# Second block of a three-part kernel: when the copies of block products stand, which steps use block products, and where the side work goes

## Chip, cores and metric

One Trainium2 chip, one core. The metric is the device time of one launch in microseconds (us). The clock of the matmul engine has two levels, 1.2 and 2.4 GHz; the profile gives the granted level as a share of the higher one.

## The reference

```python
def _attn_ref(q, k, v, g_norm):
    kv = np.einsum('bhsd,bhse->bhde', k, v)
    out = np.einsum('bhsd,bhde->bhse', q, kv)
    rms = np.sqrt(np.mean(out * out, axis=-1, keepdims=True) + 1e-06)
    return (out / rms * g_norm).astype(np.float32)

def _moe_ref(x, w_in, w_out):
    h = x @ w_in
    g = np.maximum(0.01 * h, h)
    return (g @ w_out).astype(np.float32)

def _moe2_ref(x, w_in, w_out, a, b):
    h = x @ w_in
    h2 = h * h
    h3 = h2 * h
    P = a[0] + a[1] * h + a[2] * h2 + a[3] * h3
    Q = 1.0 + np.abs(b[0]) * np.abs(h) + np.abs(b[1]) * h2
    g = P / (Q + 1e-06)
    return (g @ w_out).astype(np.float32)
```

The result of the attention part (batch 8, 8 heads, 576 positions, head size 64), laid out as 4608 rows of 512, goes through `_moe_ref` (the first block, inner width 2048) and then through `_moe2_ref` (the second block, the same widths). All is float32.

## The kernel before

**Tiling.** The 4608 rows are 9 chunks `c` of 512. The inner width of 2048 is 16 slices `f` of 128. Every float32 operand is held as a pair of float16 values, high and low, and a product is three float16 matmuls (`mm3`, L433 to L435). An instruction order written out by hand is kept on every engine; a wait between engines is set wherever an instruction touches a tile that another engine wrote or read.

**The second block** (L1313 to the end) runs 9 chunks of 8 steps `j`; a step makes slices 2j and 2j+1 of `h` in one accumulator tile of two banks, `ph` (two such tiles in turn), then the rational function `g` of them. It also runs one pair of slices of the second matmul, `y`, from a step made earlier: `y_steps2(n)` takes n pieces off a list `pend` as long as it holds more than `lag` slices. A piece is 3 matmuls of 512 columns, and 8 pieces are a pair of slices.

**The rational function** (`rational`, L1316) is, on ScalarE (ACT), three reads of `ph` into `e`, `s`, `p` (L1324 to L1326), and `z` (two instructions, L1332 and L1333); on VectorE (DVE), `d1` (L1335, from `s` and `e`), `d2` and `d3` (L1337, L1338, from `p` and `ph`), and `d4` to `d6` (L1339 to L1341, from `e`, `z`, `p`). Its last part `g` is a high half by ScalarE (L302) and a low half by GpSimd (POOL, L297).

**Plain and block steps.** A plain step makes `h` by 24 matmuls of 512 columns (`emit_h`, twice 12). A block step (`by_parts`, odd `j`) makes it out of seven block products in the manner of Strassen and Winograd, each 6 matmuls of 256 columns. The text numbers them in their order: 1 is A11 x B11, 2 is A12 x B21, 3 is S2 x T2, 4 is S1 x T1, 5 is S3 x T3, 6 is S4 x B22, 7 is A22 x T4. Four quarters `q0` to `q3` of the tile `ph` take them (`q0`, `q1` in the first bank, `q2`, `q3` in the second): products 1, 3, 5 and 7 go to `q0`, product 2 to `q2`, 4 and 6 to `q3`. ScalarE copies `q0` after product 1 (`m`, L1511) and after 3 (`u`, L1518), and `q3` after product 4 (`v`, L1522). VectorE then adds `m` to `q2` (L1515), `v` and `q0` into `q1` (L1526), and `u` to `q3` (L1532). Block steps before: j = 5 and 7 of chunk 1, and all odd steps of chunks 2 to 8 but the last of all: 29.

In a block step the code stands as follows, with `r` the rational function of the plain step before it:

```python
product2(q0, j, kc, "A11", "B11", True)
nc.scalar.copy(out=m, in_=q0)
product2(q2, j, kc, "A12", "B21", True)
y_steps2(3)
run(r, "z d2")
nc.vector.tensor_tensor(out=q2, in0=m, in1=q2, op=ALU.add)
run(r, "d3")
```

The rational function of the block step itself (`fresh`) is run in the plain step that follows.

**Side work.** Block steps need sums of the operands: of the weights, per odd j, a load (`load_sums`), four sums on VectorE (`sum_w2`, L1412) and two conversions (`form_w2`); of the next chunk's rows, four sums `T1` to `T4` (L1453) with four conversions on each of ScalarE and VectorE (`H`, `L`, L350 and L352), besides the conversions of the rows themselves (`h`, `l`, same lines). `plan` says at which step each is put. The scales of the last chunk (`x_scales`, L238 to L292, 14 short parts that go back and forth between ScalarE and VectorE) all stand at step 6 of chunk 1.

Of the kernel before, what the change touches and what calls it, by code (L numbers as in the profile page):

```python
# [9 lines left out]
F32 = mybir.dt.float32  # L10
# [10 lines left out]
P = 128  # L21
# [27 lines left out]
def kernel(  # L49
# [489 lines left out]
    with tc.manual_schedule():  # L539
# [809 lines left out]
        steps, evac, fresh, half, late = [], [], [], [], []  # L1349

        def y_steps2(n):
            for _ in range(n):
# [6 lines left out]
                if pf == p0 and e == 0:  # L1359
                    assert not evac  # L1360
                    Y[pc] = new_y()
# [97 lines left out]
        FILLS = ("h0 T1", "h1 l0 T2 T3", "h2 h3 l1", "H1 H2 l2 l3 T4", "H3 L1", "H4 L2 L3", "L4")  # L1459
# [4 lines left out]

        for c in range(NCH - 1):
            for n, f in enumerate(FILLS):
                for x in f.split():
                    put(c, min(n + (2 if c == 0 else 1), NP - 1), x[0] not in "hH", x_item, c + 1, x)
        for j, c, n in ((5, 0, 1), (7, 0, 3), (1, 1, 0), (3, 1, 2)):
            for i in range(2):  # L1470
                put(c, n + i * (c == 0), 1, sum_w2, j, i)
            for i in range(2):
                put(c, n + 1 + (c == 0) + i, i, form_w2, j, i)
        ask_w2 = {(0, 0): 5, (0, 1): 7, (0, 6): 1, (1, 0): 3}
# [5 lines left out]
        def by_parts(c, j):  # L1480
            return j % 2 and (c > 1 or c == 1 and j > 4) and (c, j) != (NCH - 1, NP - 1)

        lag = 4
        for c in range(NCH):
            kc = NCH + c
            if c == 1:
                lag = 6
            for j in range(NP):
                ph = ps_h2.tile([P, 2, N], F32, tag="h2", name="ph2")
# [3 lines left out]
                if final:  # L1493
                    late.pop(0)["g"](False)
                    for i in range(2):
                        if i:
                            ph = ps_h2.tile([P, 2, N], F32, tag="h2", name="ph2")
                        emit_h(2 * j + i, ph[:, i, :], X[kc], W2)
                        r = rational(c, ph, gt, i, i + 1)
# [65 lines left out]
                if c == 1 and j == 3:  # L1565
                    asked = spread_sums(x_norms(NCH - 1, 1), dqx, 1)
                if c == 1 and j == 6:
                    reduce(wrk["n"][:, NCH - 1:NCH], asked, ALU.add)
                    for *_, fn in x_scales(wrk["n"][:, NCH - 1:NCH], NCH - 1, 1):
                        fn()  # L1570
# [49 lines left out]
```

## Time and profile before

| | |
|---|---|
| median of 3 runs | 1604.55 us (1603.87 to 1605.08) |
| profiled execution: its time | 1603.33 us |
| its span, first to last instruction | 1601.5 us |
| PE / DVE / ACT / POOL busy | 1545.5 / 1223.5 / 990.3 / 190.1 us |
| mean granted clock | 0.993 |
| chain that ended last | PE 61%, DVE 23%, ACT 8%, DMA 4% |

Busy times are sums over an engine's instructions. PE is the matmul engine. Its busy share of 97% counts slow and overlapped matmuls too, so what it loses is read from the stretches in which it started nothing, and from the starts of its steps.

### The profile page before, as it was taken

To read this page: it belongs to the slowest core of one execution; us is meant where nothing else is said; L and a number is where in the kernel's file an instruction comes from. 1 tells how busy PE (TensorE), PEld (TensorE's weight loads), DVE (VectorE), ACT (ScalarE), POOL (GpSimd) and SP (SyncE) were. 2 spreads that over 40 slices of the span, in tenths; PEclk is the share of its full clock that TensorE was granted. 3 is DMA by queue.
4 is the path that set the end of the run, shared out by engine and by line. 5 is a ranking of instruction groups with operands and counts; after the bars stand their busy time and mean duration, and the time that the engine had idled before them with its cause. 6 is when DMAs were issued, how large, how long until landed. Compare 5 with 4: busy or idle time off the path is not lost.

```text
span 1601.5 us, 22684 instructions
## 1 busy us (share of the span) xinstructions
PE 1545.5 (97%) x9156; PEld 901.8 (56%) x9156; DVE 1223.5 (76%) x1658; ACT 990.3 (62%) x1404; POOL 190.1 (12%) x136
## 2 busy tenths in 40 slices
PE   9999999999999999999999978999999999999998
PEld 5888754445666666666644434555555555555553
DVE  6787466766765767665679998989889898989776
ACT  6567645544545555545767666767677776767665
POOL 0000000000110101000011221122221221222220
PEclk9999999999999999999999989999999999999999
DMA  8454623140534434323321010101010100100000
GB/s 320 120 185 148 172 95 93 66 119 21 186 126 125 158 116 128 100 85 106 118 79 55 1 55 1 53 1 53 1 53 1 42 12 7 47 1 27 1 27 27
DMA packets 44205, 125.26 MB, mean 78 GB/s; under 512 B 4932, under 2 KB 5316, under 8 KB 44100
## 3 DMA queue, kind: packets, MB, share of 16 engines
q1 hardware_dynamic: 35936, 96.42, 18.3%
q0 software_dynamic: 7200, 25.69, 5.2%
q10 hardware_dynamic: 964, 1.70, 0.5%
q8 instruction: 71, 1.16, 0.3%
q14 instruction: 34, 0.28, 0.1%
HBM read 92.34 MB, written 31.46 MB: 77 GB/s over the span
## 4 chain that ended last, share of the span: by engine, by line
PE 61%; DVE 23%; ACT 8%; DMA 4%; issue 4%; SPq 0%; POOL 0%; ACTq 0%; POOLq 0%; DVEq 0%
PE y L433 10%; PE y L434 10%; PE y L435 10%; PE ph L433 6%; PE ph L435 6%; PE ph L434 6%; DVE e L1335 3%; DVE p L1338 3%; DVE p L1340 2%; DVE p L1337 2%; DVE e L1339 2%; DVE x L352 2%; DVE p L1341 2%; PE chain L433 2%; ACT g L302 2%
## 5 line engine op out<-in xcount | busy, mean ns | idle before, releaser
L297 POOL TENSOR_TENSOR g<-p,g 128x1024 f16<-128x1024 f32 x70 | 156.8, 2240 | 731.2 <-ACT g L302 712.3
L435 PE MATMUL y<-g,v 128*128 128x512 f16 x576 | 219.6, 381 | 3.4 <-POOL g L297 3.4
L433 PE MATMUL y<-g,v 128*128 128x512 f16 x576 | 220.1, 382 | 0.0
L434 PE MATMUL y<-g,v 128*128 128x512 f16 x576 | 220.0, 382 | 0.0
L433 PE MATMUL ph<-x,v 128*128 128x512 f16 (+1 forms) x460 | 162.4, 353 | 41.6 <-ACT m L1511 37.5
L434 PEld LDWEIGHTS <-v 128*128 128x128 f16 x1094 | 107.4, 98 | 140.8 <-issue 43.9
L435 PEld LDWEIGHTS <-v 128*128 128x128 f16 x1094 | 107.5, 98 | 111.9 <-issue 2.1
L433 PE MATMUL y<-g,n 128*128 128x512 f16 x448 | 169.8, 379 | 0.0
L434 PE MATMUL y<-g,n 128*128 128x512 f16 x448 | 169.8, 379 | 0.0
L435 PE MATMUL y<-g,n 128*128 128x512 f16 x448 | 169.8, 379 | 0.0
L433 PEld LDWEIGHTS <-v 128*128 128x128 f16 x1094 | 107.5, 98 | 108.9 <-issue 5.7
L435 PE MATMUL ph<-x,v 128*128 128x512 f16 (+1 forms) x460 | 162.5, 353 | 0.0
L434 PE MATMUL ph<-x,v 128*128 128x512 f16 (+1 forms) x460 | 162.5, 353 | 0.0
L302 ACT ACTIVATE g<-p 128x1024 f16<-128x1024 f32 (+1 forms) x73 | 76.5, 1047 | 97.5 <-DVE p L1341 97.3
L435 PEld LDWEIGHTS <-n 128*128 128x128 f16 x816 | 79.7, 98 | 70.8
L1335 DVE SCALAR_TENSOR_TENSOR e<-s,b,e 128x1024 f32<-128x1024 f32 (+1 forms) x73 | 97.8, 1340 | 26.4 <-ACT s L1325 26.4
L433 PEld LDWEIGHTS <-n 128*128 128x128 f16 x816 | 79.9, 98 | 61.9 <-issue 5.6
L1332 ACT ACTIVATE z<-e,lnb 128x1024 f32<-128x1024 f32 (+1 forms) x73 | 83.1, 1138 | 47.3 <-DVE e L1335 47.1
L434 PEld LDWEIGHTS <-n 128*128 128x128 f16 x816 | 79.7, 98 | 56.8 <-issue 0.7
L1324 ACT ACTIVATE e<-ph,small 128x1024 f32<-128x1024 f32 (+1 forms) x73 | 79.7, 1092 | 31.7 <-DVE ph L1532 28.8
L1338 DVE SCALAR_TENSOR_TENSOR p<-p,small,ph 128x1024 f32<-128x1024 f32 (+1 forms) x73 | 92.3, 1264 | 1.6
L1340 DVE SCALAR_TENSOR_TENSOR p<-p,small,z 128x1024 f32<-128x1024 f32 (+1 forms) x73 | 92.3, 1264 | 0.0
(252 smaller groups left out, 3425.2 us busy)
## 6 DMA issues: line engine op xcount, KB each, us to landing
tmp<-in_w_dram SPq DMA_DIRECT2D x32, 512.0 KB, 7.1
raw<-in_kv_dram SPq DMA_DIRECT2D x25, 512.0 KB, 5.5
w<-in_w_dram POOLq DMA_DIRECT2D x22, 512.0 KB, 5.2
w<-cv SPq DMA_DIRECT2D x32, 256.0 KB, 3.2
raw<-w SPq DMA_DIRECT2D x16, 512.0 KB, 4.1
raw<-x SPq DMA_DIRECT2D x16, 512.0 KB, 4.3
out_dram<-raw SPq DMA_DIRECT2D x16, 512.0 KB, 2.9
sq<-rs SPq DMA_DIRECT2D x13, 512.0 KB, 6.6
```

Of the source, the lines that this page charges most:

```text
L297: (nc.gpsimd if pool else nc.vector).tensor_tensor(out=lo, in0=src, in1=hi if hi.dtype == F16 else hi.bitcast(F32), op=ALU.subtract)
L302: nc.scalar.activation(out=hi, in_=src, func=AF.Copy)
L352: nc.vector.scalar_tensor_tensor(out=lo, in0=src, scalar=scale, in1=hi, op0=ALU.mult, op1=ALU.subtract)
L433: nc.tensor.matmul(out=dst, lhsT=wl, rhs=xh, start=first, stop=False, **kw)
L434: nc.tensor.matmul(out=dst, lhsT=wh, rhs=xh, start=False, stop=False, **kw)
L435: nc.tensor.matmul(out=dst, lhsT=wh, rhs=xl, start=False, stop=last, **kw)
L1324: nc.scalar.activation(out=e, in_=ph, func=AF.Abs, scale=k["e"])
L1332: nc.scalar.activation(out=z[0], in_=e, func=AF.Abs_reciprocal_sqrt, scale=Q_S, bias=lnb[:, 1:2])
L1335: return {"d1": lambda: stt(out=e, in0=s, scalar=b1[:, 0:1], in1=e, op0=ALU.mult, op1=ALU.add), "z": root, "d2": lambda: nc.vector.tensor_ ...
L1337: "d2": lambda: nc.vector.tensor_tensor(out=p, in0=p, in1=ph, op=ALU.mult),
L1338: "d3": lambda: stt(out=p, in0=p, scalar=k["c1"], in1=ph, op0=ALU.add, op1=ALU.mult),
L1340: "d5": lambda: stt(out=p, in0=p, scalar=k["c0"], in1=z[0], op0=ALU.add, op1=ALU.mult),
```

## The change

Five things change, all in the second block.

1. In a block step the copies `m`, `u` and `v` are issued behind the next product: `m` behind product 2, and `u` and `v` together behind product 4, which now follows product 3 at once. The tile `vm` holds `v` and `m`, and one addition of 512 columns makes `q1` and `q2` behind product 5.
2. The `g` of a plain step that a block step follows moves from that block step into the plain step after it, behind `e`, `s`, `p`; there the conversions on ScalarE (`fill(c, j, 0)`) move behind `z`.
3. Block steps are used from chunk 2 on: 27. The sums of the rows of chunk 1 (`T`, `H`, `L`) are left out.
4. Side work: all weight sums and their loads stand in chunk 0, the norm of the last chunk is asked for at step 3 of chunk 0, and its 14 scale parts stand one to a step in chunks 2 and 3. The evacuation of the first block's last chunk (`after`) stands at the end of its step.
5. `lag` goes 4, 5, 6 where it went 4, 6, and in the last step 4 pieces of `y` stand behind each of the two `h`.

```diff
@@ y_steps2
-                    evac_y(ys, x2[pc], (nc.scalar, nc.scalar), x=pc, scale=sy1)
+                    after.append(lambda: evac_y(ys, x2[pc], (nc.scalar, nc.scalar), x=pc, scale=sy1))
@@ plan
-        for j, c, n in ((5, 0, 1), (7, 0, 3), (1, 1, 0), (3, 1, 2)):
+        for j, n in ((1, 0), (3, 1), (5, 3), (7, 4)):
...
+        put(0, 3, 1, last_norms)
+        put(0, 7, 1, sum_norms)
+        for i, (v, _, fn) in enumerate(x_scales(wrk["n"][:, NCH - 1:NCH], NCH - 1, 1)):
+            put(2 + i // NP, i % NP, v > 0, fn)
...
         def by_parts(c, j):
-            return j % 2 and (c > 1 or c == 1 and j > 4) and (c, j) != (NCH - 1, NP - 1)
+            return j % 2 and c > 1 and (c, j) != (NCH - 1, NP - 1)
...
+                lag = 4 if c == 0 else 5 if (c, j) == (1, 0) else 6
@@ last step
                         emit_h(2 * j + i, ph[:, i, :], X[kc], W2)
+                        y_steps2(NC)
...
-                    y_steps2(2 * NC)
@@ block step
-                    product2(q0, j, kc, "A11", "B11", True)
-                    nc.scalar.copy(out=m, in_=q0)
-                    product2(q2, j, kc, "A12", "B21", True)
+                    product2(q[:, 0, :], j, kc, "A11", "B11", True)
+                    product2(q[:, 2, :], j, kc, "A12", "B21", True)
+                    nc.scalar.copy(out=vm[:, 1, :], in_=q[:, 0, :])
                     y_steps2(3)
-                    run(r, "z d2")
-                    nc.vector.tensor_tensor(out=q2, in0=m, in1=q2, op=ALU.add)
-                    run(r, "d3")
-                    product2(q0, j, kc, "S2", "T2")
-                    nc.scalar.copy(out=u, in_=q0)
-                    y_steps2(1)
+                    run(r, "z d2 d3")
+                    product2(q[:, 0, :], j, kc, "S2", "T2")
+                    product2(q[:, 3, :], j, kc, "S1", "T1", True)
+                    nc.scalar.copy(out=u, in_=q[:, 0, :])
+                    nc.scalar.copy(out=vm[:, 0, :], in_=q[:, 3, :])
+                    y_steps2(2)
                     fill(c, j, 0)
-                    product2(q3, j, kc, "S1", "T1", True)
-                    nc.scalar.copy(out=v, in_=q3)
-                    y_steps2(1)
                     run(r, "d4 d5")
-                    product2(q0, j, kc, "S3", "T3")
-                    nc.vector.tensor_tensor(out=q1, in0=v, in1=q0, op=ALU.add)
+                    product2(q[:, 0, :], j, kc, "S3", "T3")
+                    nc.vector.tensor_tensor(out=q[:, 1:3, :], in0=vm, in1=ph[:, :, 0:HN], op=ALU.add)
...
-                    run(r, "d6 g")
+                    run(r, "d6")
+                    late.append(r)
                     fill(c, j, 1)
@@ plain step behind a block step
                         r = rational(*fresh.pop())
-                        fill(c, j, 0)
-                        fill(c, j, 1)
-                        run(r, "d1 " + REST)
+                        late.pop(0)["g"]()
+                        fill(c, j, 1)
+                        run(r, "d1 z")
+                        fill(c, j, 0)
+                        run(r, "d2 d3 d4 d5 d6")
```

On PE, where product 1 ends and product 2 begins, step 5 of chunk 2, before (`ph` is the accumulator, `x` the rows, `v` the weights):

```order
L435 LDWEIGHTS v_7354
L435 MATMUL ph_9178<-x_1_8213,v_7354 128x256
L433 LDWEIGHTS v_7354
L433 MATMUL ph_9178<-x_2_8214,v_7354 128x256 [waits Activation_49]
L434 LDWEIGHTS v_7354
```

and now:

```order
L435 LDWEIGHTS v_7354
L435 MATMUL ph_9080<-x_1_8211,v_7354 128x256
L433 LDWEIGHTS v_7354
L433 MATMUL ph_9080<-x_2_8212,v_7354 128x256
L434 LDWEIGHTS v_7354
```

Product 2 waited for ScalarE and no longer does. Three `y` pieces later, product 3 now has the wait:

```order
L435 MATMUL y_8919<-g_8812,v_7000 128x512
L433 LDWEIGHTS s_5_7951
L433 MATMUL ph_9080<-x2T_8440,s_5_7951 128x256 [waits Activation_49]
L434 LDWEIGHTS s_5_7951
L434 MATMUL ph_9080<-x2T_8440,s_5_7951 128x256
```

On ACT, steps 4 and 5 of chunk 2, before (`x2T` are conversions of sums of rows):

```order
L1326 ACTIVATE p<-ph_9001,small 128x1024 [waits Pool_49]
L350 ACTIVATE x2T_9129<-xsum,small 128x512
L350 ACTIVATE x2T_9131<-xsum,small 128x512
L1332 ACTIVATE z<-e,lnb 128x1024 [waits DVE_49]
...
L302 ACTIVATE g_9002<-p 128x1024 [waits DVE_49]
L1511 COPY m<-ph_9178 128x256 [waits PE_49]
L1332 ACTIVATE z<-e,lnb 128x1024 [waits DVE_49]
L1333 ACTIVATE z<-z 128x1024 [waits Activation_49]
L1518 COPY u<-ph_9178 128x256 [waits DVE_49,PE_49]
L350 ACTIVATE x2T_9221<-xsum,small 128x512
L1522 COPY v<-ph_9178 128x256 [waits PE_49]
L302 ACTIVATE g_9096<-p 128x1024 [waits DVE_49]
```

and now:

```order
L1326 ACTIVATE p<-ph_8900,small 128x1024 [waits Pool_49]
L302 ACTIVATE g_8812<-p 128x1024
L1332 ACTIVATE z<-e,lnb 128x1024 [waits DVE_49]
L1333 ACTIVATE z<-z 128x1024 [waits Activation_49]
L350 ACTIVATE x2T_9037<-xsum,small 128x512
...
L302 ACTIVATE g_8901<-p 128x1024 [waits DVE_49]
L1527 COPY vm<-ph_9080 128x256 [waits PE_49]
L1332 ACTIVATE z<-e,lnb 128x1024 [waits DVE_49]
L1333 ACTIVATE z<-z 128x1024 [waits Activation_49]
L1532 COPY u<-ph_9080 128x256 [waits PE_49]
L1533 COPY vm<-ph_9080 128x256
L350 ACTIVATE x2T_9131<-xsum,small 128x512
```

The `g` of the plain step before has moved ahead of `z`, the conversions behind it, and the two copies `u` and `v` stand together, still behind the next `z`.

## Rows read from the trace of the kernel before

**Rows 1.** Busy time by stretch: us, then PE, PEld, DVE, ACT, POOL, clock, DMA.
```profile
801.80:987.20 185.40, 165.74 (x780) 77.58 (x781) 169.91 (x182) 120.55 (x134) 31.87 (x15) 0.94 0.11 39
987.20:1570.40 583.20, 559.06 (x3129) 305.67 (x3127) 501.40 (x499) 416.24 (x476) 122.75 (x55) 1.00 0.07 22
1570.40:1601.50 31.10, 26.20 (x121) 11.50 (x119) 18.88 (x23) 13.55 (x19) 2.15 (x1) 0.99 0.09 34
```
**Rows 2.** Who waited for whom, 987.2 to 1570.4: total us, times, longest.
```profile
DVE ph L1532 <- PE ph L435: 29.2, 28, 1.6
...
PE ph L433 <- ACT m L1511: 24.1, 27, 1.5
```
**Rows 3.** Who waited for whom, 801.8 to 987.2.
```profile
PE ph L433 <- ACT m L1511: 13.3, 2, 6.8
...
PE y L435 <- POOL g L297: 3.4, 2, 2.0
...
PE ph L433 <- DVE p L1338: 2.9, 3, 2.1
```
**Rows 4.** Timeline of PE, chunk 2: start, us, idle before and its end.
```profile
1018.86 0.27 PE L435 MATMUL ph<-x,v 128*128 128x256 f16 x1
1020.61 0.27 PE L433 MATMUL ph<-x,v 128*128 128x256 f16 x1 [1.48 <-ACT m L1511]
...
1029.88 0.38 PE L433 MATMUL ph<-x,v 128*128 128x512 f16 x1
...
1040.24 0.27 PE L433 MATMUL ph<-x,v 128*128 128x256 f16 x1
...
```
**Rows 5.** Timeline of ACT, steps 4 and 5 of chunk 2.
```profile
1032.55 1.21 ACT L1326 ACTIVATE p<-ph,small 128x1024 f32<-128x1024 f32 x1
1033.64 1.34 ACT L350 ACTIVATE x2T<-xsum,small 128x512 f16<-128x512 f32 x2
1034.87 1.15 ACT L1332 ACTIVATE z<-e,lnb 128x1024 f32<-128x1024 f32 x1
...
1040.88 1.06 ACT L302 ACTIVATE g<-p 128x1024 f16<-128x1024 f32 x1 [0.68 <-DVE p L1341]
1041.85 0.35 ACT L1511 COPY m<-ph 128x256 f32<-128x256 f32 x1
1042.10 1.15 ACT L1332 ACTIVATE z<-e,lnb 128x1024 f32<-128x1024 f32 x1
...
1045.70 0.37 ACT L1518 COPY u<-ph 128x256 f32<-128x256 f32 x1 [1.36 <-PE ph L435]
```
**Rows 6.** Timeline of ACT, steps 2 and 3 of chunk 2.
```profile
1020.17 0.39 ACT L1511 COPY m<-ph 128x256 f32<-128x256 f32 x1
1021.41 1.15 ACT L1332 ACTIVATE z<-e,lnb 128x1024 f32<-128x1024 f32 x1 [0.85 <-DVE e L1335]
```
**Rows 7.** Timeline of DVE, chunk 2.
```profile
1030.42 2.60 DVE L352 SCALAR_TENSOR_TENSOR x<-raw,small,x 128x512 f16<-128x512 f32 x2
...
1040.77 1.28 DVE L1335 SCALAR_TENSOR_TENSOR e<-s,b,e 128x1024 f32<-128x1024 f32 x1
```
**Rows 8.** Timeline of POOL and of DVE beside it, chunk 0, then chunk 2.
```profile
845.66 2.21 POOL L297 TENSOR_TENSOR g<-p,g 128x1024 f16<-128x1024 f32 x1 [8.29 <-ACT g L302]
...
845.81 3.15 DVE L1335 SCALAR_TENSOR_TENSOR e<-s,b,e 128x1024 f32<-128x1024 f32 x1
...
1042.07 2.13 POOL L297 TENSOR_TENSOR g<-p,g 128x1024 f16<-128x1024 f32 x1 [10.27 <-ACT g L302]
```
**Rows 9.** DVE by line, 801.8 to 987.2: busy us, mean ns.
```profile
L1335 DVE SCALAR_TENSOR_TENSOR e<-s,b,e 128x1024 f32<-128x1024 f32 x15 | 24.8, 1652 | 4.5 <-ACT s L1325 4.5
...
L352 DVE SCALAR_TENSOR_TENSOR x2T<-xsum,small,x2T 128x512 f16<-128x512 f32 x8 | 8.8, 1131 | 0.0
...
L1526 DVE TENSOR_TENSOR ph<-v,ph 128x256 f32<-128x256 f32 x2 | 0.9, 430 | 0.6 <-PE ph L435 0.6
```
**Rows 10.** Timeline of PE in the last step.
```profile
1573.84 0.39 PE L433 MATMUL ph<-x,v 128*128 128x512 f16 x1 [0.73 <-DVE p L1338]
```

More of the change, by code (lines that the diff above doesn't have):

```diff
@@ L1348 @@
         REST = "z d2 d3 d4 d5 d6"
-        steps, evac, fresh, half, late = [], [], [], [], []
+        steps, evac, fresh, half, late, after = [], [], [], [], [], []
         def y_steps2(n):
@@ L1359, in y_steps2 @@
                 if pf == p0 and e == 0:
-                    assert not evac
+                    assert not evac and not after
                     Y[pc] = new_y()
@@ L1457, in x_item @@
             split16(t[:, 0, :], t[:, 1, :], stage["t", i][:, (n - 1) % 2, :], col["sx"][:, c:c + 1], int(kind == "L"))
-        FILLS = ("h0 T1", "h1 l0 T2 T3", "h2 h3 l1", "H1 H2 l2 l3 T4", "H3 L1", "H4 L2 L3", "L4")
+        FILLS = {1: "h0 T1", 2: "h1 l0 T2", 3: "h2 h3 l1 T3", 4: "H1 H2 l2 l3 T4", 5: "H3 L1", 6: "H4 L2 L3", 7: "L4"}
         plan = {}
@@ L1463, in put, with last_norms, sum_norms @@
             plan.setdefault((c, j), ([], []))[vector].append(lambda: fn(*args))
+        def last_norms():
+            x = x_norms(NCH - 1, 1)
+            t = wp.tile([P, 2, N], F32, tag=stage["tags"][0], name="asked").rearrange("p a n -> p (a n)")[:, 0:P]
+            nc.sync.dma_start(out=dqx.rearrange("k p -> p k"), in_=x)
+            nc.sync.dma_start(out=t, in_=dqx.to_broadcast([P, P]))
+            stage["asked"] = t
+        def sum_norms():
+            reduce(wrk["n"][:, NCH - 1:NCH], stage["asked"], ALU.add)
         for c in range(NCH - 1):
-            for n, f in enumerate(FILLS):
+            for j, f in FILLS.items():
                 for x in f.split():
-                    put(c, min(n + (2 if c == 0 else 1), NP - 1), x[0] not in "hH", x_item, c + 1, x)
-        for j, c, n in ((5, 0, 1), (7, 0, 3), (1, 1, 0), (3, 1, 2)):
+                    if c or x[0] in "hl":
+                        put(c, max(j, 2) if c == 0 else j, x[0] not in "hH", x_item, c + 1, x)
+        for j, n in ((1, 0), (3, 1), (5, 3), (7, 4)):
             for i in range(2):
-                put(c, n + i * (c == 0), 1, sum_w2, j, i)
+                put(0, n + 1, 1, sum_w2, j, i)
             for i in range(2):
-                put(c, n + 1 + (c == 0) + i, i, form_w2, j, i)
-        ask_w2 = {(0, 0): 5, (0, 1): 7, (0, 6): 1, (1, 0): 3}
+                put(0, n + 2 + i, i, form_w2, j, i)
+        put(0, 3, 1, last_norms)
+        put(0, 7, 1, sum_norms)
+        for i, (v, _, fn) in enumerate(x_scales(wrk["n"][:, NCH - 1:NCH], NCH - 1, 1)):
+            put(2 + i // NP, i % NP, v > 0, fn)
+        ask_w2 = {(0, 0): 3, (0, 1): 5, (0, 2): 7}
         def fill(c, j, vector):
@@ L1485 @@
             kc = NCH + c
-            if c == 1:
-                lag = 6
             for j in range(NP):
+                lag = 4 if c == 0 else 5 if (c, j) == (1, 0) else 6
                 ph = ps_h2.tile([P, 2, N], F32, tag="h2", name="ph2")
@@ L1504 @@
                     late.pop(0)["g"](False)
-                    y_steps2(2 * NC)
                 elif by_parts(c, j):
                     r = half.pop()
-                    q0, q1, q2, q3 = (ph[:, i // 2, i % 2 * HN:(i % 2 + 1) * HN] for i in range(4))
-                    m, u, v = (tb.tile([P, HN], F32, tag=x, name=x, bufs=1) for x in "muv")
-                    product2(q0, j, kc, "A11", "B11", True)
-                    nc.scalar.copy(out=m, in_=q0)
-                    product2(q2, j, kc, "A12", "B21", True)
@@ L1513 @@
-                    y_steps2(3)
-                    run(r, "z d2")
-                    nc.vector.tensor_tensor(out=q2, in0=m, in1=q2, op=ALU.add)
-                    run(r, "d3")
-                    product2(q0, j, kc, "S2", "T2")
-                    nc.scalar.copy(out=u, in_=q0)
-                    y_steps2(1)
+                    q = ph.rearrange("p a (b n) -> p (a b) n", b=2)
+                    t = [tb.tile([P, 2, HN], F32, tag=x, name=x, bufs=1) for x in ("vm", "u")]
+                    vm, u = t[0], t[1][:, 0, :]
@@ L1527 @@
                     y_steps2(3)
-                    product2(q3, j, kc, "S4", "B22")
-                    product2(q0, j, kc, "A22", "T4")
-                    run(r, "d6 g")
+                    product2(q[:, 3, :], j, kc, "S4", "B22")
+                    product2(q[:, 0, :], j, kc, "A22", "T4")
+                    run(r, "d6")
+                    late.append(r)
                     fill(c, j, 1)
-                    nc.vector.tensor_tensor(out=q3, in0=u, in1=q3, op=ALU.add)
+                    nc.vector.tensor_tensor(out=q[:, 3, :], in0=u, in1=q[:, 3, :], op=ALU.add)
@@ L1560 @@
                         fill(c, j, 1)
+                    while after:
+                        after.pop()()
                 if c == 0 and j < 2:
@@ L1564 @@
                     chore["w2"] = load_w2(NF - 1) if j == 0 else None
[L1565 to L1570, printed above, removed]
+                if (c, j) == (0, 0):
+                    load_sums(1)
                 if (c, j) in ask_w2:
```

## Prediction

> **What bounds the kernel now.** I read the busy times by stretch first, with the cuts where the second block begins, where its chunk 2 begins and where its last step begins. The first block, up to 801.8 us, is not touched. The stretch of chunks 0 and 1 takes 185.4 us and has a granted clock of 0.94, the stretch of chunks 2 to 8 without the last step takes 583.2 us at 1.00, the rest 31.1 us [rows 1]. PE looks busy in all of them, so its loss is read from step starts: a plain step runs from 1029.88 to 1040.24, 10.36 us for 48 matmuls of 512 columns, 0.216 us each at the full clock of 2.4 GHz [rows 4]. A matmul of 256 columns is then 0.108 us, and a block step (42 of those, 24 of 512) 9.71 us if nothing holds it.
>
> Chunks 2 to 8: 28 plain steps and 27 block steps make 28 x 10.36 + 27 x 9.71 = 552.3 us, against 583.2. The list of waits names the holder: PE waits for the copy `m` 27 times, 24.1 us [rows 2], once in each block step. The timeline shows the place: the last matmul of product 1 starts at 1018.86 and the first of product 2 at 1020.61, when 0.11 us would do; of these 1.64 us the view counts 1.48 as idle, so each wait costs 0.16 us more than it shows [rows 4]. That is 24.1 + 27 x 0.16 = 28.4 us. `m` itself is late because ScalarE first does the `g` of the step before, which waits for the end of VectorE's chain [rows 5]; VectorE is not full here: it waits 29.2 us for the last block products alone [rows 2].
>
> Chunks 0 and 1: after the change all 16 steps are plain, less one pair of `y` put off as the lag grows (5.18 us): 16 x 10.36 - 5.18 = 160.6 us, against 185.4. The waits are the two block steps of chunk 1 (13.3 us, one of 6.8 us), and 3.4 and 2.9 us for `g` and for the release of `ph` [rows 3]; the rest of the 24.8 us is work at the lower clock of 1.2 GHz, which the rows show only in this stretch and at the end [rows 1]. VectorE is busy 169.9 of the 185.4 us, and part of that is waiting inside its instructions [rows 1, 8].
>
> **The change part by part.**
>
> *Copies behind the next product.* Product 2 has no wait any more; the wait for `m` stands at product 3, behind product 2 (0.65 us) and three `y` pieces (1.94 us). So `m` may end 2.59 us after product 1. In step 5 product 1 ends at 1040.24 + 0.65 = 1040.89 and `m` at 1042.20 [rows 4, 5]: 1.28 us to spare. In step 3, which has `y` to evacuate before, it ends at 1018.86 + 0.11 = 1018.97 and `m` at 1020.56 [rows 4, 6]: 1.00 us to spare. The change also moves work ahead of `m` on ScalarE: the `g` that now stands before `z` starts at about 1033.64, where conversions stood for 1.34 us, and lets `z` go 0.97 us later (the distance from `g` to `m`), at 1034.6 in place of 1034.87 [rows 5]. The conversions come behind `z` now, 0.62 us each, two of them before step 5 and one before step 3; 0.68 us is covered by the idle time before the next `g` in step 5, and I count on no cover in step 3. So `m` moves by some 0.3 and 0.6 us, and 1.0 and 0.4 us stay to spare: the wait is gone from there.
>
> *`u` and `v` together.* Product 5 now waits for both, and they stand behind the next `z` on ScalarE. Without other waits product 5 starts 5.18 us after product 1, at 1046.07 in step 5. `u` there waited for PE, not for `z` (1.36 us [rows 5]); issued behind product 4, whose last matmul ends near 1045.0, it leaves `v` done two copies of 0.37 us later, at 1045.7: 0.4 us to spare. In step 3 `z` starts at 1021.41 [rows 6]; with its two parts of 1.15 us and two copies `v` ends at 1024.3 or 1024.4, against 1018.97 + 5.18 = 1024.15: 0.2 us short. The addition of 512 columns is not in the trace: it lies between the 0.43 us of one of 256 columns [rows 9] and 0.86, two of them. I take 0.7, since a fixed part is paid once. It must end before product 6, 2.59 us after product 5, and in step 3 that has nothing to spare either.
>
> *`g` in the plain step.* In the block step it is gone; what waited for it is `y` three steps on, so nothing waits now. Where POOL ran it, it held up VectorE's conversions at the start of the plain step, 2.60 us for two [rows 7]; half of 1.34 us is what ScalarE takes for one [rows 5], so more than 1 us of VectorE's chain is gained there.
>
> So in chunks 2 to 8 at most 28.4 us go, and what comes back lies in the steps 3 and 5 of a chunk, with their fuller side work, and in the 14 scale parts of chunks 2 and 3: I take 0.4 us per chunk of 2 to 7 and 1 us for the scales, **3.4 us** together. Ends of the range: nothing, and half of the 28.4. This part: **-25.0 us**.
>
> *Chunks 0 and 1.* Two block steps become plain, +1.3 us of PE work (in the 160.6 already). The two waits for `m` go, and the scale chain in which VectorE and ScalarE hand small pieces back and forth goes to places where one part per step has 10 us. Four sums, four conversions on each engine for chunk 1 go (VectorE's part of the conversions is half of 8.8 us, and the sums are four of 0.43 us at least [rows 9]), and with the block steps six additions, 2.6 us; the weight sums of two more `j` only move into chunk 0. VectorE's need falls from 169.9 by these 8.7 us and a little for the scale parts, to about 160 us, against PE's 160.6: almost full. In it is time lost to POOL (15 `d1` at 1.65 us in place of 1.28 [rows 7, 9] alone are 5.6 us). A plain step leaves VectorE some 2.9 us beside its six instructions of 1.2 to 1.3 us; step 1 of chunk 0 gets some 5.6 us of side work (four sums of 0.43, two reductions of 1024 columns, two conversions) and step 4 some 4.4 us. Added up over chunk 0, VectorE falls behind by up to 7 to 8 us; a pair of slices made in step j is needed in the second half of step j + 2, which allows 7.2 us. So a stall of 0 to 2.5 us, and one near the short steps where the lag grows; I take **3 us**, with ends of 0 and 12. The evacuation behind the step's other work takes away the first wait for `g`. DMAs: the weight loads move ahead on SP's queue to a place where PE's last use of the tile has gone by; what is queued behind them, rows of the next chunk, is needed a step later. This part: 160.6 + 3 - 185.4 = **-21.8 us**.
>
> *Last step.* The wait of 0.73 us [rows 10] (0.9 from start to start) before the second half goes, as `y` stands there: **-0.9 us**. The `lag` of 5 in one step moves work only.
>
> Sum: -25.0 - 21.8 - 0.9 = -47.7 us on the profiled execution's 1603.33, which lies 1.2 us under the median: 1555.6, or **1556.8** as a median.
>
> **A rule against the change.** A `d1` that came while POOL's `g` ran took 3.15 us in place of 1.28 [rows 7, 8]; `d2`, with an operand in `ph`, was never long. The Trainium skill (SBUF - State Buffer, section "SBUF: two separate sides") says that the port pair VectorE and GpSimd share is a lock that whichever starts first holds for its whole instruction, and that a VectorE instruction with two SBUF inputs needs it. By that rule, with which these rows agree, the moved `g` could stop `d1` in every plain step; it is the third rival.
>
> **The rivals.**
> 1. *The wait comes back at product 5 or 3* (15%). For it: `u` and `v` stand behind `z`, and step 3 has no time to spare. Against it: steps 1, 5 and 7 have. If half of the 28.4 us stays, 14.2 in place of the 3.4 that I took, the time is 1556.8 + 10.8 = 1568.
> 2. *Chunk 0 is full* (10%): VectorE's need stays above PE's; 12 us of stall in place of 3: 1566.
> 3. *`d1` behind POOL* (3%), slower. If `g` reaches POOL before `d1` starts, in the plain and in the block step, `d1` costs 1.87 us more, 3.74 per pair of steps. With 0.8 us to spare, PE then stalls 2.9 us per pair, 79 us in 27, in place of 28.4: 1604.55 + 51 - 22.7 = 1633. It decides if `d1` starts later than the end of ScalarE's `g`. Now `d1` starts at 1040.77, 1.3 us ahead of POOL [rows 7, 8], and in the plain step `d1` needs `s`, one instruction earlier than the `g` that comes behind `p`.
> 4. *Product 2 still waits for something as late as `m`* (2%): only chunks 0 and 1 and the end gain, 1604.55 - 22.7 = 1582. The order shows no other wait there.
>
> **How the numbers follow.** The forecast gets 70%, its own range 1550 (nothing comes back) to 1563. The range of 1550 to 1572 takes in rivals 1 and 2. A difference of 0.2% (3 us) is what a measurement of this kernel can tell from no change. All cases but the third lie below: faster 0.95, slower 0.03, the same 0.02.
>
> **What would show it.** Right: PE's wait for the copies falls from 24.1 to under 4 us and stands before product 3 or 5; the stretch of chunks 2 to 8 takes about 558 us and that of chunks 0 and 1 about 164 at a clock near 1.00; the two waits of 6.8 and 6.6 us have no successor. Wrong: instructions of 3.1 us at `d1` in chunks 2 to 8 (rival 3), a total wait of over 10 us for `u` or `v` (rival 1), or waits for `g` and `ph` above 6 us in chunk 0 (rival 2).

## The result and the profile after

The changed kernel takes **1548.9 us** (median of 4 runs, 1548.13 to 1549.74) against 1604.3 (4 runs, 1603.87 to 1605.08): ratio 0.9654, 95% interval 0.9638 to 0.9671. The gain is 55.4 us where 47.7 was forecast. The direction and the place were right; the time lies 7.9 us under the forecast and 1.1 us under the range's lower end of 1550.

The busy times by stretch of the profile after, with the cuts at the same places of the program as in [rows 1] (columns as there):

```profile
802.00:962.70 160.70, 160.67 (x744) 72.73 (x745) 148.86 (x143) 118.68 (x123) 35.96 (x15) 1.00 0.13 45
962.70:1516.60 553.90, 553.90 (x3128) 305.82 (x3126) 483.83 (x497) 404.92 (x477) 118.71 (x55) 1.00 0.07 24
1516.60:1546.90 30.30, 26.15 (x122) 11.64 (x119) 19.53 (x24) 13.78 (x19) 2.14 (x1) 0.97 0.10 35
```

Of the profiled executions (1603.33 and 1548.73 us) the parts compare so, with the starts of step 0 of chunk 0 (802.03), of step 0 of chunk 2 (962.78) and of the last step (1516.68) as cuts:

| stretch | before | after | gain | forecast |
|---|---|---|---|---|
| chunks 0 and 1 | 185.4 | 160.75 | 24.65 | 21.8 |
| chunks 2 to 8 without the last step | 583.2 | 553.9 | 29.3 | 25.0 |
| last step to the end | 31.1 | 30.2 | 0.9 | 0.9 |

The list of PE's waits from 802.0 to the end now has one row, at the seam of the two blocks, where [rows 2] and [rows 3] had 24.1, 13.3, 3.4 and 2.9 us:

```profile
PE ph L433 <- DVE hq L1303: 0.5, 1, 0.5
```

PE's timeline in step 3 of chunk 2, the fuller kind of block step, answers to [rows 4]; the rows are the starts of products 1, 3 and 5, of the last two matmuls before product 6, of product 6 and of the next plain step:

```profile
993.26 0.27 PE L433 MATMUL ph<-x,v 128*128 128x256 f16 x1
...
996.51 0.27 PE L433 MATMUL ph<-x2T,s 128*128 128x256 f16 x1
...
999.12 0.27 PE L433 MATMUL ph<-x2T,s 128*128 128x256 f16 x1
...
1001.29 0.38 PE L434 MATMUL y<-g,v 128*128 128x512 f16 x1
1001.50 0.38 PE L435 MATMUL y<-g,v 128*128 128x512 f16 x1
1001.72 0.27 PE L433 MATMUL ph<-x,s 128*128 128x256 f16 x1
...
1003.03 0.38 PE L433 MATMUL ph<-x,v 128*128 128x512 f16 x1
```

No row has an idle time, and the chain that ended last is PE for 90% where it was 61%. The step takes 9.77 us, 0.06 more than the 9.71 of its matmuls. ScalarE in the same step, beside [rows 6]:

```profile
995.54 0.39 ACT L1527 COPY vm<-ph 128x256 f32<-128x256 f32 x1
996.11 1.15 ACT L1332 ACTIVATE z<-e,lnb 128x1024 f32<-128x1024 f32 x1 [0.18 <-DVE e L1335]
997.29 1.06 ACT L1333 ACTIVATE z<-z 128x1024 f32<-128x1024 f32 x1
998.26 0.35 ACT L1532 COPY u<-ph 128x256 f32<-128x256 f32 x1
998.51 0.38 ACT L1533 COPY vm<-ph 128x256 f32<-128x256 f32 x1
```

and VectorE:

```profile
1000.78 0.69 DVE L1538 TENSOR_TENSOR ph<-vm,ph 128x512 f32<-128x512 f32 x1
```

`m` ends at 995.93, 0.58 us before product 3; `v` at 998.89, 0.23 before product 5; the addition at 1001.47, 0.25 before product 6. Read in the same way for all 27 block steps, the room in us is

| step | m before 3 | v before 5 | addition before 6 |
|---|---|---|---|
| 1 and 7 (in chunk 3, step 7 has 0.83, 0.45 and 0.80) | 1.37 | 0.45 | 0.98 |
| 3, chunks 2 to 7 | 0.58 | 0.23 | 0.25 |
| 5, chunks 4 to 7 | 0.59 | 0.45 | 0.60 |
| 5, chunks 2 and 3 | 0.05 | 0.05 | 0.12 |
| 3 and 5 of chunk 8 | 1.19 and 1.37 | 0.23 and 0.45 | 0.25 and 0.98 |

In the steps 5 of chunks 2 and 3, two steps with scale parts beside the fuller side work, products 3 and 5 start as soon as they may; each step loses 0.08 us by it.

### The profile page after: what moved, and what is told of

Same layout as the page of the kernel before. It is cut to its first block, busy times and chain, and to the rows that moved or that the text cites. A ratio compares the mean times of both kernels' runs of the same rounds, so it can differ in the third digit from the quotient of the medians.

```text
span 1546.9 us, 22520 instructions
## 1 busy us (share of the span) xinstructions
PE 1534.7 (99%) x9120; PEld 897.1 (58%) x9120; DVE 1185.5 (77%) x1617; ACT 977.5 (63%) x1394; POOL 190.2 (12%) x136
## 4 chain that ended last, share of the span: by engine, by line
PE 90%; DMA 4%; DVE 4%; ACT 1%; issue 1%; SPq 0%; ACTq 0%; DVEq 0%
PE y L433 15%; PE y L435 15%; PE y L434 15%; PE ph L433 11%; PE ph L435 11%; PE ph L434 11%; PE chain L433 2%; DMA w<-cv 2%; PE chain L435 2%; PE chain L434 2%; PE other L433 1%; PE other L435 1%; PE other L434 1%; PE kvacc L579 1%; DMA raw<-in_kv_dram 1%; PE po L596 1%
## 5 line engine op out<-in xcount | busy, mean ns | idle before, releaser
L433 PE MATMUL ph<-x,v 128*128 128x512 f16 (+1 forms) x468 | 165.9, 354 | 0.5 <-DVE hq L1303 0.5
L434 PE MATMUL ph<-x,v 128*128 128x512 f16 (+1 forms) x468 | 165.9, 354 | 0.0
L435 PE MATMUL ph<-x,v 128*128 128x512 f16 (+1 forms) x468 | 165.9, 354 | 0.0
L1339 DVE SCALAR_TENSOR_TENSOR e<-e,z 128x1024 f32<-128x1024 f32 (+1 forms) x73 | 88.5, 1212 | 19.9 <-ACT z L1333 18.5
```

Of the source, the lines that this page charges most:

```text
L433: nc.tensor.matmul(out=dst, lhsT=wl, rhs=xh, start=first, stop=False, **kw)
L434: nc.tensor.matmul(out=dst, lhsT=wh, rhs=xh, start=False, stop=False, **kw)
L435: nc.tensor.matmul(out=dst, lhsT=wh, rhs=xl, start=False, stop=last, **kw)
L1339: "d4": lambda: stt(out=e, in0=e, scalar=Q_C, in1=z[0], op0=ALU.add, op1=ALU.mult),
```

## The experiments

Twelve kernels were run with three rounds each (4 runs). The kernel before had medians of 1604.5 to 1604.8 beside them. Times by stretch are from step starts in each trace, with the same cuts as above.

| kernel | median us (lowest to highest) | chunks 0, 1 | chunks 2 to 8 |
|---|---|---|---|
| after | 1548.9 (1548.1 to 1549.7) | 160.75 | 553.9 |
| e1 parts 1 and 2 alone | 1573.39 (1571.2 to 1576.9) | 183.5 | 555.0 |
| e2 parts 3 to 5 alone | 1583.17 (1583.1 to 1583.4) | 160.7 | 588.3 |
| e13 `m` ahead | 1587.15 (1586.1 to 1588.7) | 160.7 | 591.9 |
| e4 additions apart | 1556.32 (1556.2 to 1556.6) | 160.7 | 561.3 |
| e11 two late additions | 1549.60 (1548.9 to 1550.6) | 160.7 | 554.5 |
| e3 `g` back | 1553.24 (1552.2 to 1553.5) | 160.7 | 557.8 |
| e7 `g` between | 1567.10 (1565.4 to 1568.0) | 160.7 | 572.1 |
| e5 ScalarE dose | 1553.08 (1552.9 to 1553.9) | 160.7 | 558.1 |
| e8 scales spread | 1565.58 (1565.2 to 1566.3) | 175.9 | 553.7 |
| e12 no blocks in chunk 1 | 1551.75 (1551.4 to 1555.1) | 162.2 | 553.7 |
| e10 evacuation first | 1552.49 (1552.2 to 1554.7) | 164.4 | 553.9 |
| e9 VectorE dose | 1554.56 (1553.2 to 1555.8) | 166.4 | 553.9 |

### Which part brings which time

**e1.** The kernel before with the new block step and the moved `g` (parts 1 and 2), nothing else.

```diff
...
-                    nc.scalar.copy(out=m, in_=q0)
-                    product2(q2, j, kc, "A12", "B21", True)
+                    product2(q[:, 2, :], j, kc, "A12", "B21", True)
+                    nc.scalar.copy(out=vm[:, 1, :], in_=q[:, 0, :])
...
-                    run(r, "d6 g")
+                    run(r, "d6")
+                    late.append(r)
...
```

> The kernel before with parts 1 and 2 of the change alone: the new block step, and g moved into the plain step. Side work, scale parts, block steps of chunk 1 and lag as before. Theory A (each part removes its own wait and needs no other): chunks 2 to 8 without the last step fall from 583.2 to about 554 us as in the changed kernel; in chunk 1 the two waits for m of 6.9 and 6.7 us shrink by 2.5 us each (product 2 and three y pieces now cover them), 180 in place of 185.4. Time 1566 to 1573. Theory B (the copies alone leave waits at products 3 and 5, and the new places of the side work give the room): over 3.4 us of waits in chunks 2 to 8, time above 1576.

Theory A in chunks 2 to 8: they gain 28.1 of their 29.3 us without the new plan, no wait of PE is left there, and the time is 0.4 us above the range. The missing 1.3 us stand in the first of their steps, a plain one that takes 11.66 us where 10.36 would do: PE has waited 3.0 and 2.1 us in the block step before it, and the granted clock falls to 0.52 for some 3 us.

```profile
985.00:988.00 3.00, 3.00 (x12) 1.37 (x10) 1.39 (x3) 1.38 (x2) 0.00 (x0) 0.52 0.00 0
```

Chunks 0 and 1 gain 2.0 us, not the 5 expected: in the two block steps of chunk 1 the waits moved on to products 3 and 6. (The 184.8 us that a later expectation gives for this stretch counts the 1.3 us at the lower clock into it.) The list of waits from 802 to 990 (`vm` at L1513 is `m`; L1524 is the addition, for which product 6 waits):

```profile
PE ph L433 <- ACT vm L1513: 5.5, 2, 3.0
PE ph L433 <- DVE ph L1524: 5.2, 2, 3.1
PE ph L433 <- DVE p L1338: 4.4, 4, 2.1
PE y L435 <- POOL g L297: 3.4, 2, 2.0
```

**e2.** The changed kernel with the old block step and the old place of `g`.

```diff
...
-                    product2(q[:, 2, :], j, kc, "A12", "B21", True)
-                    nc.scalar.copy(out=vm[:, 1, :], in_=q[:, 0, :])
+                    nc.scalar.copy(out=m, in_=q0)
+                    product2(q2, j, kc, "A12", "B21", True)
...
-                    run(r, "d6")
-                    late.append(r)
+                    run(r, "d6 g")
...
```

> The changed kernel with the old block step and the old place of g: parts 3, 4 and 5 alone. Theory A: chunks 0 and 1 take 160.7 us as in the changed kernel (185.4 before) and the last step gains 0.9, chunks 2 to 8 stay at 583, with up to 3 us more where the 14 scale parts now stand ahead of m in chunks 2 and 3: 1578 to 1582. Theory B (chunks 0 and 1 gain only with the new block step behind them): above 1585.

Theory A, 1.2 us above its range: chunks 0 and 1 gain all of their 24.7 us, and chunks 2 to 8 lose 5.1 where up to 3 were expected. The old block step waits longest, 2.99 us, where the scale parts now stand.

```profile
PE ph L433 <- ACT m L1525: 25.8, 27, 3.0
```

The gains of e1 and e2, 31.1 and 21.3 us, add up to 52.4 of 55.4: the parts are nearly independent. What is missing lies mostly where they meet: scale parts in an old block step cost 5.1 us that the new one hides.

**e13.** In the changed kernel `m` alone goes ahead of product 2.

```diff
-                    product2(q[:, 2, :], j, kc, "A12", "B21", True)
                     nc.scalar.copy(out=vm[:, 1, :], in_=q[:, 0, :])
+                    product2(q[:, 2, :], j, kc, "A12", "B21", True)
```

> The changed kernel with m alone issued ahead of product 2 again, all the rest kept. Theory A (the place of m is what the wait in the block step hangs on): product 2 waits 0.6 us in steps 1 and 7 and 1.4 to 2 us in steps 3 and 5, together 27 to 37 us: 1575 to 1586. Theory B (with g moved and one addition, ScalarE would be in time for m anyway): under 0.5 us a step, 1549 to 1562.

Theory A, 1 us above its range: PE waits in each of the 27 steps, 38.0 us in all. The block step is slower than the old one (step 3 waits 2.06 us from start to start where it waited 1.64). By the order of the instructions the moved `g` now stands ahead of `m` in the plain step before; no run separates this from the other moves.

```profile
PE ph L433 <- ACT vm L1526: 33.8, 27, 1.9
```

### Which piece of the block step

**e4.** Two additions of 256 columns, `m`'s between `d2` and `d3` as before.

```diff
-                    run(r, "z d2 d3")
+                    run(r, "z d2")
+                    nc.vector.tensor_tensor(out=q[:, 2, :], in0=vm[:, 1, :], in1=q[:, 2, :], op=ALU.add)
+                    run(r, "d3")
...
-                    nc.vector.tensor_tensor(out=q[:, 1:3, :], in0=vm, in1=ph[:, :, 0:HN], op=ALU.add)
+                    nc.vector.tensor_tensor(out=q[:, 1, :], in0=vm[:, 0, :], in1=q[:, 0, :], op=ALU.add)
```

> The changed kernel with two additions of 256 columns in place of the one of 512: m to q2 between d2 and d3 as before, v and q0 behind product 5. Theory A (the fused addition has 1.7 us to spare before product 6, so it was worth nothing on PE): 1549, within 1.5 us, VectorE busier by 27 times 0.43 + 0.43 - 0.69 = 4.6 us. Theory B (VectorE's chain in the block step sets g and with it the next step's m): the 0.43 us put ahead of d3 come back in the steps with 0.23 us to spare at product 5, 7 to 14 of them by 0.2 us: 1550 to 1552.

Neither theory: 7.4 us. (The 1.7 us in the expectation was misread from the record of the addition's semaphore wait; the addition's own row has 0.25 in step 3.) The list of waits, and VectorE and PE in step 3 of chunk 2:

```profile
PE ph L433 <- DVE ph L1530: 6.5, 7, 0.9
```

```profile
993.55 1.40 DVE L1391 TENSOR_SCALAR raw<-y,small 128x512 f32<-128x512 f32 x2
994.87 1.27 DVE L1335 SCALAR_TENSOR_TENSOR e<-s,b,e 128x1024 f32<-128x1024 f32 x1
996.07 1.21 DVE L1337 TENSOR_TENSOR p<-p,ph 128x1024 f32<-128x1024 f32 x1
997.20 0.42 DVE L1530 TENSOR_TENSOR ph<-vm,ph 128x256 f32<-128x256 f32 x1
```

```profile
997.67 0.27 PE L433 MATMUL ph<-x2T,s 128*128 128x256 f16 x1 [0.92 <-DVE ph L1530]
```

Product 3 writes `q0` and the addition `q2`, but the wait is set by the tile `ph`. In step 3 the two evacuations of `y` on VectorE (L1391) stand ahead of `d1`. `m` is there at 996.00, but its addition follows `d2` and starts only at 997.20; the step takes 1.08 us more, in each of seven chunks.

**e11.** Two additions again, both behind product 5.

```diff
-                    nc.vector.tensor_tensor(out=q[:, 1:3, :], in0=vm, in1=ph[:, :, 0:HN], op=ALU.add)
+                    for i in range(2):
+                        nc.vector.tensor_tensor(out=q[:, 1 + i, :], in0=vm[:, i, :], in1=ph[:, i, 0:HN], op=ALU.add)
```

> The changed kernel with two additions of 256 columns, both behind product 5, where the change has one of 512. Theory A (what cost 7.4 us with the additions apart was that the addition of m stood ahead of d3, and product 3 had to wait for it since it touches the tile; the number of additions is nothing): no wait before product 3, 1549 within 1 us. Theory B (one instruction in place of two is what counts, 0.2 us less VectorE work per block step against 0.2 us of room): 1552 to 1556.

Theory A: the list of waits shows none. It is the place of `m`'s addition that is worth 7 us. Making one instruction of two is worth 0.7 us at most: the trace has 0.3 us each in the steps 5 of chunks 2 and 3, and the ranges of the two kernels' runs overlap.

**e3.** Part 2 undone.

```diff
-                    run(r, "d6")
-                    late.append(r)
+                    run(r, "d6 g")
...
-                        late.pop(0)["g"]()
-                        fill(c, j, 1)
-                        run(r, "d1 z")
-                        fill(c, j, 0)
-                        run(r, "d2 d3 d4 d5 d6")
+                        fill(c, j, 0)
+                        fill(c, j, 1)
+                        run(r, "d1 " + REST)
```

> The changed kernel with part 2 undone: g of the plain step stands in the block step again, and the conversions on both engines ahead of d1. Theory A (the move of g is a matter of order and hides no wait): 1549, within 2 us. Theory B (the room in steps 3, 5 and 7 comes from it): conversions locked behind POOL make VectorE's chain 1.2 us later, against 0.23 to 0.45 us to spare at product 5 and 0.58 at product 3, so 0.3 to 1 us of wait in three of four block steps: 20 waits, 1555 to 1568, standing at products 3 and 5 of steps 3, 5 and 7.

Between the two: 4.3 us, in four steps and not 20 (the list names three waits). They are the steps 3 and 5 of chunks 2 and 3, where the scale parts have taken the room; in the other chunks nothing waits for the place of `g`.

```profile
PE ph L433 <- ACT vm L1527: 3.0, 2, 1.6
...
PE ph L433 <- ACT vm L1533: 0.2, 1, 0.2
```

**e7.** The moved `g` between `e` and `s`, one place earlier.

```diff
...
             nc.scalar.activation(out=e, in_=ph, func=AF.Abs, scale=k["e"])
+            if mid:
+                mid()
...
-                        r = rational(*fresh.pop())
-                        late.pop(0)["g"]()
+                        r = rational(*fresh.pop(), mid=late.pop(0)["g"])
```

> The changed kernel with the moved g (27 of them) one place earlier on ScalarE, between e and s of the block step's function, so that POOL's part starts before d1 can. Theory A (VectorE and POOL shut each other out while both inputs lie in SBUF): d1 of the block step's function takes 2.3 to 3.2 us in place of 1.28, and 1 to 1.9 us more per pair of steps against 0.2 to 0.6 us of room give waits in 20 to 27 block steps: 1560 to 1590. Theory B (no lock; POOL and VectorE run side by side): d1 stays at 1.28 us, 1549 to 1553.

Theory A: `d1` (here L1337) has a mean of 1795 ns over 54, in the changed kernel 1280; with half of them at 1.28 us the other 27 take 2.3. The timeline shows one: it ends 1.08 us after POOL. PE loses more than 0.1 us in 15 block steps (20 to 27 were expected), mostly in waits for `m` and, in `y`, for an evacuation on ScalarE.

```profile
L1337 DVE SCALAR_TENSOR_TENSOR e<-s,b,e 128x1024 f32<-128x1024 f32 x54 | 97.0, 1795 | 57.1 <-ACT s L1327 57.1
```

```profile
1009.92 2.30 DVE L1337 SCALAR_TENSOR_TENSOR e<-s,b,e 128x1024 f32<-128x1024 f32 x1 [1.22 <-ACT s L1327]
```

```profile
1009.01 2.13 POOL L297 TENSOR_TENSOR g<-p,g 128x1024 f16<-128x1024 f32 x1 [8.72 <-ACT g L302]
```

```profile
PE ph L433 <- ACT vm L1529: 7.2, 8, 1.4
PE y L433 <- ACT raw L1396: 5.5, 7, 0.9
```

So 1 us on `d1`, and an `s` and a `p` that come an instruction later, cost 18.2 us together; no run tells the shares of the two apart. The long `d1` is the third rival's mechanism at work, in one of the two steps of a pair.

### How much room there is

**e5.** Two further copies on ScalarE ahead of `m`.

```diff
+                    for _ in range(2):
+                        nc.scalar.copy(out=t[1][:, 1, :], in_=q[:, 0, :])
                     nc.scalar.copy(out=vm[:, 1, :], in_=q[:, 0, :])
```

> The changed kernel with two further copies of 128x256 on ScalarE ahead of m in each of the 27 block steps, 0.27 us each from start to start, 0.54 together (they write an unused half of a tile). Theory A (the room read from the changed kernel's trace is real: m has 1.37, 0.58, 0.59 and 1.37 us to spare in steps 1, 3, 5, 7, u and v 0.45, 0.23, 0.45 and 0.45, and 0.05 in step 5 of chunks 2 and 3): about 0.3 us of wait at product 5 in the seven steps 3 and 0.5 to 1 us in two steps 5, none in steps 1 and 7: 1552 to 1554. Theory B (the room is larger, something else sets when products 3 and 5 start): 1549, within 1 us.

Theory A: 4.2 us. `m` is issued 0.67 us later (2.18 us after the step's start in step 1, where it was 1.51); steps 1 and 7 lose nothing, step 3 of chunk 2 takes 0.2 us more and step 5 0.8 (0.33 in chunks 4 to 7). The room in the table above is what PE goes by: in step 3 product 3 starts 0.15 us later, and 0.67 us less the 0.53 between its room of 0.58 and the 0.05 at which it starts as soon as it may are 0.14. The list of waits has two of them:

```profile
PE ph L433 <- ACT vm L1529: 1.3, 2, 0.7
```

**e9.** Five further conversions on VectorE in step 2 of chunk 0.

```diff
+        for _ in range(5):
+            put(0, 2, 1, x_item, 1, "l0")
```

> The changed kernel with one conversion on VectorE (128x512, 0.67 us from start to start) done five times more in step 2 of chunk 0: 3.35 us more VectorE work. Theory A (VectorE has no idle time from step 2 of chunk 0 to step 1 of chunk 1, and the tightest g ends 0.5 us before its y, so chunk 0 was within 0.5 us of a stall): PE stalls 2.9 us, more or less by the 1.87 us of a d1 that falls in or out of POOL's time: 1550.5 to 1554. Theory B (several us of room, as the two steps between g and y allow): 1549, within 1 us.

Theory A, a little above its range: 5.6 us, because the five took 5.64 us and not 3.35, one of them held beside POOL:

```profile
844.73 5.64 DVE L352 SCALAR_TENSOR_TENSOR x<-raw,small,x 128x512 f16<-128x512 f32 x5
```

```profile
845.05 2.41 POOL L297 TENSOR_TENSOR g<-p,g 128x1024 f16<-128x1024 f32 x1 [9.73 <-ACT g L302]
```

```profile
PE y L435 <- POOL g L297: 3.4, 3, 2.2
PE ph L433 <- DVE p L1338: 0.8, 1, 0.8
PE y L433 <- ACT g L302: 0.7, 1, 0.7
```

All of the added VectorE time is paid by PE: VectorE is busy 5.4 us longer in the stretch, and the stretch is 5.6 us longer. So chunk 0 has under 1 us of room.

### Chunks 0 and 1

**e8.** e1 with the scale parts spread over chunks 2 and 3.

```diff
-                    for *_, fn in x_scales(wrk["n"][:, NCH - 1:NCH], NCH - 1, 1):
-                        fn()
...
+        for i, (v, _, fn) in enumerate(x_scales(wrk["n"][:, NCH - 1:NCH], NCH - 1, 1)):
+            put(2 + i // NP, i % NP, v > 0, fn)
```

> The first experiment (parts 1 and 2 alone) with the 14 scale parts one to a step in chunks 2 and 3, as the change has them; the block steps of chunk 1 stay. Theory A (the scale chain in step 6 of chunk 1 makes the waits of 2.3 to 3.2 us in the two block steps of that chunk): chunks 0 and 1 fall from 184.8 to 173 to 177 us, time 1562 to 1566. Theory B (the block steps in a chunk that is already full make them): four waits stay, 1571 to 1574.

Theory A: 7.6 us of the stretch go, and the 1.3 us at the lower clock behind it; the time falls by 7.8. One block step still waits long:

```profile
PE ph L433 <- ACT vm L1515: 4.2, 1, 4.2
PE ph L433 <- DVE p L1338: 4.1, 4, 2.1
PE y L435 <- POOL g L297: 3.5, 2, 2.0
PE ph L433 <- DVE ph L1526: 1.5, 1, 1.5
```

**e12.** e8 without block steps in chunk 1 and without the sums of its rows.

```diff
-            return j % 2 and (c > 1 or c == 1 and j > 4) and (c, j) != (NCH - 1, NP - 1)
+            return j % 2 and c > 1 and (c, j) != (NCH - 1, NP - 1)
...
-                    put(c, min(n + (2 if c == 0 else 1), NP - 1), x[0] not in "hH", x_item, c + 1, x)
+                    if c or x[0] in "hl":
+                        put(c, min(n + (2 if c == 0 else 1), NP - 1), x[0] not in "hH", x_item, c + 1, x)
```

> The kernel of the third to last expectation with scales spread (parts 1 and 2, scale parts one to a step), now also without block steps in chunk 1 and without the sums of that chunk's rows; the weight sums of two j stay in chunk 1, and evacuation and lag as before. Theory A (of the 176 us of chunks 0 and 1 there, block steps in a full chunk cost 10 to 12): 164 to 166 us, time 1553 to 1556. Theory B (the weight sums in chunk 1 and the lag are what costs): 170 us or more, above 1559.

More than theory A: 13.7 us of the stretch go. What is left against the changed kernel is one wait of `y` for `g`, 1.64 us from start to start near 828, and the one in the last step:

```profile
PE y L435 <- POOL g L297: 1.5, 1, 1.5
PE ph L433 <- DVE p L1338: 1.2, 1, 1.2
```

So all weight sums in chunk 0, the early request for the norm and the `lag` of 5 are worth nothing on PE. The same holds for one move that the list of the change leaves out: in `plan` the sum `T3` stands a step later than before. e1, e8 and e12 have it in its old place, and no step of chunks 2 to 8 waits for it there.

**e10.** The changed kernel with the evacuation ahead again.

```diff
-                    after.append(lambda: evac_y(ys, x2[pc], (nc.scalar, nc.scalar), x=pc, scale=sy1))
+                    evac_y(ys, x2[pc], (nc.scalar, nc.scalar), x=pc, scale=sy1)
```

> The changed kernel with the evacuation of the first block's last chunk where it stood before, ahead of the step's other work. Theory A (its two copies on ScalarE made g of the first pair late): the wait of y for g near 828 us is back with 1.65 us, 1550 to 1552. Theory B (the wait went because of the later places of the side work): 1549, within 1 us.

Theory A in kind: the gap near 828 is back with 1.65 us, but 3.6 us are lost in all, in further waits of 0.5 to 1.0 us later in a full chunk. In e12, with less in chunk 0, the same gap stayed alone.

```profile
PE y L435 <- POOL g L297: 2.3, 3, 1.5
PE ph L433 <- DVE p L1338: 0.8, 1, 0.8
```

## Why the prediction was right in direction and too high

**What bounded the kernel: right.** The new block step with the moved `g` gains 28.1 us (e1), and in the new step the place of `m` alone is worth 38.0 (e13). The account from matmul counts (552.3 and 160.6 us) was met to 1.6 and 0.15 us, and the clock shows 1.00 in both stretches, where chunks 0 and 1 had 0.94.

**Copies behind the next product: mechanism right, the reserve wrong.** The step that failed is "what comes back lies in the steps 3 and 5 of a chunk ... I take 0.4 us per chunk of 2 to 7 and 1 us for the scales, 3.4 us together". It measured nothing that the list of waits shows. With 2.5 us of smaller gaps left in the sum, of which 1.6 stayed, that is the 4.3 us. (One of these gaps: before, six of the steps 3 also lost 0.17 us ahead of product 5, 1.0 us that no list of waits shows.) `m`'s room in step 3 was put at 0.4 and is 0.58, in step 5 at 1.0 and is 0.59 (0.05 with a scale part); `v` in step 3 was put 0.2 short and has 0.23 to spare. Of that last 0.4, 0.26 comes from adding durations where the next instruction starts before the last one's row ends: `u` and `v` are 0.25 apart with 0.35 each, and the two parts of `z` take 2.15 us and not 2.30 until `u` starts; the rest is a `z` that starts 0.2 earlier after product 1. That the two scale steps lose only 0.08 us each is luck: no room is left in them. e5 shows how near it was: 0.67 us more on ScalarE costs 4.2.

**The additions: the term was missing.** I costed the fused addition against product 6 alone, with about nothing to spare in step 3 (0.25 measured). That `m`'s old addition would have taken the place of the wait before product 3, for 7.4 us, was in no term (e4). It had shown in no wait of before, where product 2 waited first. The change has the new place, so the forecast lost nothing by it.

**`g` in the plain step: right that nothing waits for it**, and its place decides in the steps 3 and 5 of chunks 2 and 3 only (e3, 4.3 us).

**Chunks 0 and 1: mechanism right, two sizes wrong.** The step that failed is "VectorE's need falls from 169.9 by these 8.7 us and a little for the scale parts, to about 160 us", and with it the 3 us of stall. VectorE is busy 148.9 us. By line, for the same stretch as [rows 9]:

```profile
L1335 DVE SCALAR_TENSOR_TENSOR e<-s,b,e 128x1024 f32<-128x1024 f32 x16 | 26.1, 1628 | 8.4 <-ACT s L1325 8.4
...
L1412 DVE TENSOR_TENSOR sum<-sum 128x256 f32<-128x256 f32 x16 | 8.6, 536 | 0.4
L352 DVE SCALAR_TENSOR_TENSOR x<-raw,small,x 128x512 f16<-128x512 f32 x8 | 5.8, 745 | 0.0
L352 DVE SCALAR_TENSOR_TENSOR s<-sum,small,s 128x1024 f16<-128x1024 f32 x4 | 5.1, 1279 | 0.0
```

The last three lines read so in the trace before, for as many instructions:

```profile
L1412 DVE TENSOR_TENSOR sum<-sum 128x256 f32<-128x256 f32 x16 | 12.4, 775 | 0.3
...
L352 DVE SCALAR_TENSOR_TENSOR x<-raw,small,x 128x512 f16<-128x512 f32 x8 | 7.7, 982 | 0.0
L352 DVE SCALAR_TENSOR_TENSOR s<-sum,small,s 128x1024 f16<-128x1024 f32 x4 | 7.0, 1745 | 0.0
```

That is 7.6 us of waiting for POOL that I had left in the need. The scale parts, "a little" in my sum, were 6.6 us there. In chunk 0, VectorE's lag behind its place in the first step peaks at 5.7 us (`d1` of step 5 starts at 867.11, that of step 0 at 809.63, with 5 steps of 10.36 between), where I had 7 to 8 against 7.2 allowed; so PE does not stall. It was close: after e9 the lag is paid by PE almost one for one. And my cause for the two long waits was incomplete: of the 24.65 us, the new block step took 2.0 (e1), spreading the scales 7.6 (e8), leaving the block steps out of chunk 1 another 13.7 (e12), the evacuation's new place 1.5. Part of the gain is work that no longer runs at 1.2 GHz: the granted clock of the stretch is 0.94 before, 0.98 in e1 and e8, 1.00 in e12 and in the changed kernel.

**Last step:** 0.9 as forecast. **From execution to median:** I added 1.2 us, and here median and profiled execution lie 0.2 apart; that is 1 us of the miss.

**The lower end.** The range began at 1550 for "nothing comes back", with "at most 28.4 us" from chunks 2 to 8. This bound was too tight: 29.3 went, since the smaller gaps were not in it. That 0.9 us and the 1 us from execution to median carry the time under the range.

**The rivals.** None came. The first sets in with 0.67 us more on ScalarE (e5, 4.2 of the 14.2 us that it put back). For the second, the one dose tried was 5.6 us on VectorE, and PE paid 5.6 (e9). The third's long `d1` is real (e7). The Trainium skill (SBUF — State Buffer, section "SBUF: two separate sides") gives the shared port pair, for the whole instruction, to whichever starts first of a VectorE instruction with two SBUF inputs and a GpSimd instruction that reads SBUF; e7's 2.30 us beside 1.28 agrees. The fourth did not come either: no row of PE's list names product 2. In the changed kernel `d1` starts ahead of POOL in chunks 2 to 8 and stays at 1.28, all 54 of them.

## What to carry to other kernels

Move a consumer's wait past independent work of the engine that waits, and then look for the second instruction that touches the same tile: where waits go by the tile, a late addition to another quarter takes the place of the wait removed. Add up room on an engine by starts of instructions in a row, not by their durations, and don't charge a wait where that sum leaves 0.1 us. Where the room is under 1 us on an engine that hardly idles, work put there is paid in full (5.6 us here, e9). Time spent waiting for another engine's port is part of a busy share, and can go when the order of the instructions changes (7.6 us here).

## What the runs showed of the hardware

A VectorE instruction with both inputs in SBUF that starts while POOL runs `g` lasts until POOL is done and then about its own time more: `d1` took 3.15 us where it started with POOL [rows 8], 2.30 where it came 0.9 us later (e7), and a group of five small conversions took 2.2 us longer (e9). Two copies of 0.35 us in a row on ScalarE start 0.25 us apart, and the addition of 512 columns takes 0.69 us where one of 256 takes 0.43. In chunk 0, where VectorE is busy nearly all the time, the evacuation ahead of the step's work brought a wait for `g` of 1.65 us back and cost 3.6 us in all (e10).
